# Weights joined in 16-bit pieces, loads of 112 rows, and one load issued later in a fused attention and gating kernel

## The chip, the cores and the metric

The kernel runs on one core of one Trainium2 chip. The metric is the device time of one execution in microseconds (us), the median of several runs; lower is better. The core has five engines that run side by side and meet at semaphores: PE (matrix products), DVE (vector), ACT (scalar functions), POOL and SP. SP issues all transfers of this kernel, in the order of its program, to 16 DMA engines.

## The reference

A linear attention with a decaying state feeds a gated layer that mixes over the positions of the sequence. Batch 4, 8 heads, 768 positions, head size 48, model width 384, inner width 1024.

```python
f = 1.0 / (1.0 + np.exp(-f_logit))
for t in range(S):
    state = f[:, :, t, :, None] * state + np.einsum('bhd,bhe->bhde', k[:, :, t], v[:, :, t])
    y[:, :, t] = np.einsum('bhd,bhde->bhe', q[:, :, t], state)
...
h = np.maximum(x @ w_in, 0.0)          # x: y with the heads side by side
u, v = h[..., :d_ff // 2], h[..., d_ff // 2:]
v_n = (v - mu) / np.sqrt(var + 1e-06)  # mean and variance over the width
v_s = np.einsum('ts,bsd->btd', w_spatial, v_n) + b_spatial[None, :, None]
return (u * v_s) @ w_out
```

## The kernel before

The sequence is cut into 24 units (4 batches by 6 stretches of 128 positions). For each unit n the attention needs f, k and q, which lie in one of three buffers `ins[n % 3]` (tile `fkq`), and v, in one of two (tile `val`). The two heads of a pair lie in rows 0 to 47 and 64 to 111 of the 128 rows of a buffer, so 112 rows are used. Products of float32 precision in the gated layer are made of a high and a low part of each factor, which takes three matrix products instead of one.

The order of all the work is written out by hand in the table `PLAN` (L44 to L115): each word is a step with its numbers, and a step's instructions go to the queues of their engines in the order of the words. Every engine works through its own queue in that order. So a word that is moved changes the order on the queue of each engine that it uses, and on no other.

The steps that matter here:

- `LF:n` (L350) loads f of unit n. For the first eight units f comes alone, as 128 positions by 384 (array `fn`); from unit 8 on one transfer brings f, k and q together. `LK:n` (L357) brings k and q of the first eight units. `LQ:n` (L361) loads v.
- `L:kind,i` (L291, written `LV`, `LU`, `LO` in the plan) loads one of six blocks of weights into a tile `words` or `late`. The weights were laid out as 64-bit integers, of which the kernel sees the low and the high 32-bit words (`parts_of`, L285): they are joined into a float32 on the chip.
- `ca` (ACT, L303) scales the high words into a third area t; `ct` (DVE, L308 to L310) then puts the bits together: it shifts the low words right by 29, shifts t left by 3 and combines it with the low words, and adds the sign bit of the high words. `ch` (ACT) and `cl` (DVE) make the high and the low part of the result.
- `k` (L399) and `q` (L403) on DVE scale k and q by the decays that `g` (L393) and `h` (L388) on ACT have made from the sums of f; `X` (L427, PE) makes the scores from them, `m` (L437, DVE) masks these, `YS` (L479, PE) multiplies them by v, and `kv` (L451, PE) adds to the state.

A load into a buffer has to wait until the earlier users of that part of it are done. SP carries these waits in its own queue: while one transfer waits there, all behind it wait as well.

For later use, the first words of the plan, and where `LK:3` stands:

```python
LF:0 constants kz LF:1 kq:1 c:0 e:0 LF:2 kq:0 c:1 LK:0 e:1 z:0 g:0 k:0 h:0 q:0 c:2 kj e:2 LV:1 z:1 LQ:0 ca:V,1
ct:V,1 X:0 w:0 h:1 g:1 LK:1 z:2 ch:V,1 m:0 k:1 YS:0 kv:0 q:1 LF:3 c:3 e:3 LV:0 r0:0 r1:0 X:1 w:1 cl:V,1 g:2 r2:0
Yq:0 z:3 fm:0 h:2 LQ:1 m:1 YS:1 kv:1 LK:3 LK:2 ys:0 k:2 q:2 ca:V,0 xt:0 X:2 LF:4 c:4 r0:1 LQ:2 r1:1 xh:0 xl:0
```

Of the kernel before, what the change touches and what calls it, by code (L numbers as in the profile page):

```python
# [11 lines left out]
F32R = mybir.dt.float32r  # L12
BF16 = mybir.dt.bfloat16
I32 = mybir.dt.int32
AF = mybir.ActivationFunctionType
ALU = mybir.AluOpType
PSUM = bass.MemoryType.PSUM

B, H, S, D = 4, 8, 768, 48
T = 128  # L20
C = 64
NU = S // T
N = B * NU
J = H // 2
DP = 112
# [4 lines left out]
P = 128  # L30
# [4 lines left out]
WB = 2 * DM  # L35
# [8 lines left out]
PLAN = """  # L44
    LF:0 constants kz LF:1 kq:1 c:0 e:0 LF:2 kq:0 c:1 LK:0 e:1 z:0 g:0 k:0 h:0 q:0 c:2 kj e:2 LV:1 z:1 LQ:0 ca:V,1
    ct:V,1 X:0 w:0 h:1 g:1 LK:1 z:2 ch:V,1 m:0 k:1 YS:0 kv:0 q:1 LF:3 c:3 e:3 LV:0 r0:0 r1:0 X:1 w:1 cl:V,1 g:2 r2:0
    Yq:0 z:3 fm:0 h:2 LQ:1 m:1 YS:1 kv:1 LK:3 LK:2 ys:0 k:2 q:2 ca:V,0 xt:0 X:2 LF:4 c:4 r0:1 LQ:2 r1:1 xh:0 xl:0
    e:4 z:4 m:2 g:3 LF:5 w:2 LK:4 r2:1 c:5 e:5 YS:2 kv:2 LQ:4 Yq:1 fm:1 h:3 ct:V,0 ys:1 ch:V,0 r0:2 q:3 z:5 g:5 g:4
    k:3 xt:1 LQ:3 LU:0 r1:2 cl:V,0 r2:2 xh:1 xl:1 X:3 w:3 Yq:2 ys:2 V:0,1 k:4 fm:2 h:4 LF:7 LF:6 q:4 X:4 m:3 YS:3
    c:6 kv:3 V:0,0 LK:5 ca:U,0 LU:1 ct:U,0 r0:3 w:4 ch:U,0 vr:0,1 xt:2 xh:2 m:4 YS:4 fm:3 r1:3 e:6 r2:3 vr:0,0 kv:4  # L50
# [107 lines left out]
def tile_kernel(ctx, tc, fkq, fn, vv, w_cv, w_spT, b_sp, out):  # L158
    nc = tc.nc
# [7 lines left out]
    def tiles(pool, name, count, shape, dtype=F32):  # L167
        return [pool.tile(shape, dtype, name=f"{name}{i}") for i in range(count)]
# [17 lines left out]
    ins = tiles(attn, "fkq", 3, [P, 3, J * T])  # L186
# [6 lines left out]
    sB = tiles(attn, "sB", 2, [DP, J * D])  # L193
    late_tile = const.tile([P, 3 * WB], I32, name="late")
    vr_tile = const.tile([P, HU, G], F32, name="vr")
# [6 lines left out]
    vns = Slots([tuple(const.tile([P, G], F32R, name=f"vn{k}{i}") for k in "hl") for i in range(6)])  # L202
    words = Slots(tiles(stage, "words", 2, [P, 3 * WB], I32))
    spat = Slots(tiles(stage, "spat", 2, [P, 2, TH]))
# [80 lines left out]
    def words_for(kind):  # L285
        return late if kind == "O" else words

    def parts_of(kind, i):
        w = words_for(kind).of((kind, i))
        low, high = (w[:, 0:2 * WB].rearrange("p (n two) -> p n two", two=2)[:, :, x] for x in range(2))  # L290
        return low, high, w[:, 2 * WB:]  # L291

    def step_L(kind, i):
        nc.sync.dma_start(
            words_for(kind).take((kind, i), 2)[:, 0:2 * WB].rearrange("p (h n) -> p h n", h=2),
            w_cv.bitcast(I32)["VUO".index(kind) * 2 + i].rearrange("h p n -> p h n"),
        )

    def step_ca(kind, i):


        low, high, t = parts_of(kind, i)
        nc.scalar.activation(t.bitcast(F32), high.bitcast(F32), AF.Copy, scale=2.0 ** -112)  # L303

    def step_ct(kind, i):

        low, high, t = parts_of(kind, i)
        nc.vector.tensor_scalar(low, low, 29, None, op0=ALU.logical_shift_right)  # L308
        nc.vector.scalar_tensor_tensor(t, t, 3, low, op0=ALU.logical_shift_left, op1=ALU.bitwise_or)
        nc.vector.scalar_tensor_tensor(t, high, -2 ** 31, t, op0=ALU.bitwise_and, op1=ALU.bitwise_or)  # L310

    def step_ch(kind, i):
        to, full = cols(kind, i)[0], view(kind, parts_of(kind, i)[2].bitcast(F32))
# [32 lines left out]
    def parts(n):  # L346
        t = ins[n % 3]
        return t[0:DP, 0], t[0:DP, 1], t[0:DP, 2]

    def step_LF(n):  # L350
        b, u = divmod(n, NU)
        if n < SUMMED:
            nc.sync.dma_start(ins[n % 3][:, 0, 0:HD], fn[n])
        else:
            nc.sync.dma_start(ins[n % 3], fkq[b, u])

    def step_LK(n):  # L357
        b, u = divmod(n, NU)
        nc.sync.dma_start(ins[n % 3][:, 1:3], fkq[b, u, :, 1:3])

    def step_LQ(n):  # L361
        b, u = divmod(n, NU)
# [6 lines left out]
    def step_e(n):  # L369
        f = ins[n % 3][:, 0, 0:HD] if n < SUMMED else parts(n)[0]  # L370
        nc.scalar.activation(f, f, AF.Exp, scale=-1.0)
        nc.scalar.activation(f, f, AF.Ln, bias=1.0)  # L372

# [10 lines left out]
    def sums(n):  # L384
        return mm.of(("z", n))[0:DP] if n < SUMMED else parts(n)[0]

    def step_h(n):
        nc.scalar.activation(Fs[n % 2], sums(n), AF.Exp, scale=-1.0)  # L388
        if n < SUMMED:
            mm.done(("z", n))  # L390

    def step_g(n):
        nc.scalar.activation(parts(n)[0], sums(n), AF.Exp)  # L393
        if n < SUMMED:
            mm.done(("z", n))
# [21 lines left out]
    low, high = slice(0, C), slice(C, P)  # L417
# [135 lines left out]
    def raw(b, u):  # L553
        if b not in WIN:
            return vrs.of((b, u))
        th, ut = divmod(u, HU)
        if (b, th) not in raws.held:
            raws.take((b, th), 4)
        return raws.of((b, th))[:, ut]
# [5 lines left out]
    def step_vr(b, u):  # L565
        th, ut = divmod(u, HU)
        sums = {"accum_out": half(b, th)["sum"][:, ut:ut + 1]} if moment(b, th) == "sums" else {}
        if b not in WIN:
            vrs.take((b, u))
        nc.scalar.activation(raw(b, u), mm.of(("v", b, u)), AF.Relu, **sums)  # L570
        mm.done(("v", b, u))
# [251 lines left out]
    count = const.tile([DP, 2], F32, name="count")  # L823
    bad = const.tile([1, 1], I32, name="bad")

# [54 lines left out]
    with tc.If(n_bad > 0) as found:  # L880
        xd = dram.tile([B, HD, S], F32, name="xd")
        with tc.tile_pool(name="steps", bufs=2) as sp:
# [5 lines left out]
            with tc.For_i(0, B) as b, tc.For_i(0, J) as j, tc.For_i(0, 2) as e:  # L888
                f, k, q = (sp.tile([D, NU, T], F32, tag="in", name="in", bufs=3) for _ in range(3))
# [7 lines left out]
                f, k, q = (t.rearrange("d u t -> d (u t)") for t in (f, k, q))  # L897
# [10 lines left out]
                for d in range(D):  # L908
                    kv = sp.tile([D, S], F32, name="kv")
# [101 lines left out]
```

## Time and profile before

| | |
|---|---|
| median of 3 runs | 344.37 us (343.79 to 344.56) |
| the profiled execution | 343.65 us |
| its span, first to last instruction | 341.9 us |
| PE busy | 327.2 us, 96% of the span |
| PE weight loads busy | 304.7 us |
| DVE busy | 251.3 us, 74% |
| ACT busy | 181.9 us, 53% |
| moved by DMA | 38.38 MB, 112 GB/s on the mean |

The span is the profiled execution without 1.7 us around it. PE is the engine with the most work, and its idle time is 14.7 us of the span. A share over the whole span hides where such idle time lies, so the rows below are taken by stretches. "issue" as a releaser means that the engine waited for nothing that the trace shows. A time in brackets at the end of a row is idle time of that engine in front of the row's first instruction, with what ended it.

### The profile page before, as it was taken

The page shows a single profiled execution, that of the slowest core. Times are in us where ns is not written, and L with a number is a line of the kernel's source. Part 1 is how long each engine was busy: PE and PEld are TensorE (multiplying, and loading weights), DVE is VectorE, ACT ScalarE, POOL GpSimd, SP SyncE. Part 2 cuts the span into 40 slices and gives each one's busy share as a digit, 9 for nine tenths or more (in the row PEclk, how much of TensorE's full clock was granted, in tenths as well). Part 3 has the DMA queues.
Part 4 walks back from the last instruction along what each step waited for, and adds up shares of the span by engine and source line. Part 5 has one row for each costly group of instructions (what it writes and reads, how often), then busy time and mean ns, then how long its engine had stood idle before and what let it go on. Part 6 is the DMA issues. An engine that isn't in the chain of part 4 may idle for free.

```text
span 341.9 us, 10491 instructions
## 1 busy us (share of the span) xinstructions
PE 327.2 (96%) x4554; PEld 304.7 (89%) x4554; DVE 251.3 (74%) x491; ACT 181.9 (53%) x369; POOL 48.2 (14%) x70
## 2 busy tenths in 40 slices
PE   4669999999999999999999999999999999999995
PEld 3557889889999999999999998899899899999995
DVE  2878888988988869765668557889998869624730
ACT  8665899685465745536435456443453444213431
POOL 3101200312120320051004042100101010001000
PEclk9999999999999999999999999999999999999998
DMA  7938578713454213243048121162200000011022
GB/s 253 353 97 269 182 271 304 252 30 138 143 157 134 83 54 110 77 157 117 2 143 265 46 85 50 46 200 104 71 1 0 2 0 0 2 46 49 23 74 98
DMA packets 16582, 38.38 MB, mean 112 GB/s; under 512 B 1552, under 2 KB 11792, under 8 KB 16528
## 3 DMA queue, kind: packets, MB, share of 16 engines
q1 hardware_dynamic: 16528, 37.62, 32.6%
q8 instruction: 38, 0.62, 0.8%
q14 instruction: 16, 0.13, 0.1%
HBM read 32.90 MB, written 4.72 MB: 110 GB/s over the span
## 4 chain that ended last, share of the span: by engine, by line
PE 93%; DMA 2%; issue 1%; DVE 1%; ACT 1%; SPq 0%; DVEq 0%
PE mm L658 15%; PE mm L644 12%; PE mm L542 12%; PE mm L797 10%; PE mm L733 7%; PE mn L733 6%; PE bp L427 6%; PE mn L797 5%; PE bp L479 4%; PE bp L491 4%; PE mn L542 3%; PE mn L644 3%; PE mm L504 3%; PE bp L451 3%; DMA words<-w_cv 2%; PE mm L382 2%
## 5 line engine op out<-in xcount | busy, mean ns | idle before, releaser
L399 DVE SCALAR_TENSOR_TENSOR fkq<-fkq 112x512 f32<-112x512 f32 x24 | 17.2, 718 | 11.4 <-ACT fkq L393 6.9
L649 ACT ACTIVATE uT<-mm 128x384 f32<-128x384 f32 x26 | 12.8, 491 | 22.8 <-PE mm L644 19.9
L779 ACT CAST gh<-uT 128x384 fp32r<-128x384 f32 x29 | 14.8, 514 | 18.3 <-DVE uT L775 13.6
L427 PE MATMUL bp<-q,fkq 48*64 48x112 f32 x768 | 23.7, 261 | 0.8 <-DVE q L403 0.6
L775 POOL TENSOR_TENSOR uT<-gt,uT 128x384 f32<-128x384 f32 x12 | 12.9, 1077 | 81.1 <-ACT uT L649 38.6
L470 POOL TENSOR_TENSOR sA<-sA,F 112x192 f32<-112x192 f32 x13 | 11.9, 916 | 85.4 <-DVE sA L465 81.2
L427 PEld LDWEIGHTS bp<-q,fkq 48*64 48x64 f32 x768 | 19.0, 133 | 4.7 <-DVE q L403 1.9
L377 DVE TENSOR_TENSOR_SCAN fkq<-runs,fkq 112x512 f32<-112x512 f32 x16 | 20.4, 1274 | 2.8 <-ACT fkq L372 2.8
L479 PEld LDWEIGHTS bp<-val,sc 64*64 64x64 f32 x768 | 14.2, 134 | 7.4 <-issue 3.5
L479 PE MATMUL bp<-val,sc 64*64 64x48 f32 x768 | 16.6, 220 | 4.1 <-DVE sc L437 2.1
L403 DVE TENSOR_TENSOR q<-fkq,F 112x512 f32<-112x512 f32 x24 | 16.5, 686 | 5.4 <-PE bp L491 4.0
L658 PE MATMUL mm<-w_sph,vnh 128*128 128x384 f32 x96 | 20.2, 345 | 0.0
L658 PE MATMUL mm<-w_sph,vnl 128*128 128x384 f32 x96 | 19.5, 338 | 0.0
L658 PE MATMUL mm<-w_spl,vnh 128*128 128x384 f32 x96 | 19.5, 338 | 0.0
L437 DVE TENSOR_TENSOR sc<-bp,mask 128x512 f32<-128x512 f32 x24 | 16.4, 683 | 3.8 <-PE bp L427 3.7
L644 PE MATMUL mm<-xTh,w_inh 128*128 128x384 f32 x78 | 18.9, 350 | 0.0
L367 POOL TENSOR_SCALAR fkq<-fkq 112x512 f32<-112x512 f32 (+1 forms) x8 | 12.4, 1550 | 40.7 <-DMA fkq<-fkq 20.6
L644 PE MATMUL mm<-xTl,w_inh 128*128 128x384 f32 x78 | 17.9, 338 | 0.0
L644 PE MATMUL mm<-xTh,w_inl 128*128 128x384 f32 x78 | 17.9, 338 | 0.0
L542 PE MATMUL mm<-w_inh,xTh 128*128 128x512 f32 x57 | 17.3, 411 | 0.0
L658 PEld LDWEIGHTS mm<-w_spl,vnh 128*128 128x128 f32 x96 | 17.1, 188 | 0.0
L658 PEld LDWEIGHTS mm<-w_sph,vnl 128*128 128x128 f32 x96 | 17.1, 188 | 0.0
(215 smaller groups left out, 900.3 us busy)
## 6 DMA issues: line engine op xcount, KB each, us to landing
fkq<-fkq SPq DMA_DIRECT2D x16, 768.0 KB, 4.9
val<-vv SPq DMA_DIRECT2D x24, 192.0 KB, 4.0
out<-osb SPq DMA_DIRECT2D x24, 192.0 KB, 2.1
fkq<-fkq SPq DMA_DIRECT2D x8, 512.0 KB, 5.7
words<-w_cv SPq DMA_DIRECT2D x4, 768.0 KB, 6.0
y<-w_spT SPq DMA_DIRECT2D x4, 576.0 KB, 5.9
fkq<-fn SPq DMA_DIRECT2D x8, 192.0 KB, 3.4
late<-w_cv SPq DMA_DIRECT2D x2, 768.0 KB, 5.9
```

Of the source, the lines that this page charges most:

```text
L377: return nc.vector.tensor_tensor_scan(f[0:DP], runs, f[0:DP], 0.0, op0=ALU.mult, op1=ALU.add)
L399: nc.vector.scalar_tensor_tensor(k, f, 1.0 / F_LEAST, k, op0=ALU.min, op1=ALU.mult)
L403: nc.vector.tensor_tensor(qs[n % 2][:, :, :, 0:C], *(x.rearrange("p (j c t) -> p j c t", c=T // C, t=C) for x in (parts(n)[2], Fs[n % 2])) ...
L427: nc.tensor.matmul(sc[to, e, cs], k[dr, at:at + C], qs[n % 2][dr, j, chunk], start=True, stop=True)
L437: nc.vector.tensor_tensor(Ss[n % 2].rearrange("p (e j t) -> p e j t", e=2, t=C), scores(n)[:, :, :, 0:C], mask.unsqueeze(1).unsqueeze(1).b ...
L479: nc.tensor.matmul(y[to, e, cs], s[rows, keys[e]], v[rows, hd], start=j == 0, stop=False, skip_group_check=True)
L542: nc.tensor.matmul(acc, xs[:, c, ut * P:(ut + 1) * P], ws[:, c, G:FF], start=i == 0, stop=i == 3 * KX - 1)
L644: nc.tensor.matmul(acc[:, 0:TH], ws[:, kx, cs], xs[:, kx, :], start=i == 0, stop=i == 3 * KX - 1)
L658: nc.tensor.matmul(acc[:, 0:TH], vns.of((b, ks))[va][:, cs], w_sp_s[wb][:, ks, th * TH:(th + 1) * TH], start=i == 0, stop=i == 3 * KS - 1,)
L733: nc.tensor.matmul(mm.of(user)[:, 0:TH], x, y, start=n == ks == 0 and i not in (3, 6, 7), stop=n == ks == 2, skip_group_check=True,)
L779: nc.scalar.copy(gs.take((b, th, c), HU)[0], uTs.of((b, th, c)))
L797: nc.tensor.matmul(acc[:, ms], gs.of((b, th, c))[ga][:, ts], w_out_s[wb][:, c, ms], start=c == cs[0] == 0 and ga == wb == 0, stop=c == cs[ ...
```

## The change

Three things change.

1. In `ct` the low 64-bit halves are seen as 16-bit pieces, four to a weight. Two one-source instructions write single pieces in place: the lowest piece becomes the second one shifted right by 13, and the second one becomes the sign bit of the highest. One two-source instruction then combines the 32-bit word made of these two pieces with t. Before, `ct` was one one-source instruction on 32-bit words and two two-source ones.
2. `LK:n`, and `LF:n` from unit 8 on, move 112 rows instead of 128; the array in memory has 112 rows per unit as well.
3. The word `LK:3` stands 12 words later, behind `LQ:2`.

```diff
-    Yq:0 z:3 fm:0 h:2 LQ:1 m:1 YS:1 kv:1 LK:3 LK:2 ys:0 k:2 q:2 ca:V,0 xt:0 X:2 LF:4 c:4 r0:1 LQ:2 r1:1 xh:0 xl:0
+    Yq:0 z:3 fm:0 h:2 LQ:1 m:1 YS:1 kv:1 LK:2 ys:0 k:2 q:2 ca:V,0 xt:0 X:2 LF:4 c:4 r0:1 LQ:2 LK:3 r1:1 xh:0 xl:0
...
     def step_ct(kind, i):
 
         low, high, t = parts_of(kind, i)
-        nc.vector.tensor_scalar(low, low, 29, None, op0=ALU.logical_shift_right)
+        pieces = words_for(kind).of((kind, i))[:, 0:2 * WB].bitcast(U16).rearrange("p (n four) -> p n four", four=4)
+        nc.vector.tensor_scalar(pieces[:, :, 0], pieces[:, :, 1], 13, None, op0=ALU.logical_shift_right)
+        nc.vector.tensor_scalar(pieces[:, :, 1], pieces[:, :, 3], 2 ** 15, None, op0=ALU.bitwise_and)
         nc.vector.scalar_tensor_tensor(t, t, 3, low, op0=ALU.logical_shift_left, op1=ALU.bitwise_or)
-        nc.vector.scalar_tensor_tensor(t, high, -2 ** 31, t, op0=ALU.bitwise_and, op1=ALU.bitwise_or)
...
         else:
-            nc.sync.dma_start(ins[n % 3], fkq[b, u])
+            nc.sync.dma_start(ins[n % 3][0:DP], fkq[b, u])
 
     def step_LK(n):
         b, u = divmod(n, NU)
-        nc.sync.dma_start(ins[n % 3][:, 1:3], fkq[b, u, :, 1:3])
+        nc.sync.dma_start(ins[n % 3][0:DP, 1:3], fkq[b, u, :, 1:3])
...
-        y = np.full((B, NU, P, J * T), pad, np.float32)
+        y = np.full((B, NU, DP, J * T), pad, np.float32)
```

On SP, from the third load of f alone into buffer 0 (`LF:3`) on, the queue stood like this before; `fkq0` to `fkq2` are the three buffers of f, k and q, `val` those of v, `words` those of weights, and 128x1024 is a load of k and q:

```order
L353 DMA fkq0_112<-fn 128x384
L294 DMA words1_160<-w_cv 128x2x768
L363 DMA val1_116<-vv 128x384
L359 DMA fkq0_112<-fkq 128x1024
L359 DMA fkq2_114<-fkq 128x1024
L353 DMA fkq1_113<-fn 128x384
L363 DMA val0_115<-vv 128x384
L353 DMA fkq2_114<-fn 128x384
L359 DMA fkq1_113<-fkq 128x1024
```

And the same place of SP's queue with the change (lines are numbered one or two higher):

```order
L355 DMA fkq0_112<-fn 128x384
L295 DMA words1_160<-w_cv 128x2x768
L365 DMA val1_116<-vv 128x384
L361 DMA fkq2_114<-fkq 112x1024
L355 DMA fkq1_113<-fn 128x384
L365 DMA val0_115<-vv 128x384
L361 DMA fkq0_112<-fkq 112x1024
L355 DMA fkq2_114<-fn 128x384
L361 DMA fkq1_113<-fkq 112x1024
```

The load of k and q of unit 3 into `fkq0` has moved from ahead of that of unit 2 (`fkq2`) to behind f of unit 4 and v of unit 2; the loads of k and q are 112 rows.

On DVE the first weights (`words0`) are joined just ahead of the mask of unit 0 (`sc0`) and of k and q of unit 1; before:

```order
L308 TENSOR_SCALAR words0_159<-words0_159 128x768
L309 SCALAR_TENSOR_TENSOR words0_159<-words0_159 128x768
L310 SCALAR_TENSOR_TENSOR words0_159<-words0_159 128x768
L437 TENSOR_TENSOR sc0_117<-bp0_138,mask_109 128x512
L399 SCALAR_TENSOR_TENSOR fkq1_113<-fkq1_113 112x512
```

With the change, in the same place of DVE's queue:

```order
L310 TENSOR_SCALAR words0_159<-words0_159 128x768
L311 TENSOR_SCALAR words0_159<-words0_159 128x768
L312 SCALAR_TENSOR_TENSOR words0_159<-words0_159 128x768
L439 TENSOR_TENSOR sc0_117<-bp0_138,mask_109 128x512
L401 SCALAR_TENSOR_TENSOR fkq1_113<-fkq1_113 112x512
```

One two-source instruction has gone and a one-source one has come; nothing else on DVE's queue moves. On PE, ACT and POOL the order is the same as before.

## Rows read from the trace of the kernel before

**Rows 1.** Busy us and instruction count of each engine, by three stretches

```profile
core 0: us, PE busy (x) PEld busy (x) DVE busy (x) ACT busy (x) POOL busy (x), PEclk, DMA share, GB/s
4.90:33.30 28.40, 22.52 (x608) 18.55 (x608) 21.20 (x37) 19.62 (x38) 4.23 (x7) 1.00 0.72 254
33.30:336.00 302.70, 302.50 (x3932) 284.13 (x3931) 228.60 (x450) 158.11 (x324) 41.80 (x51) 1.00 0.30 98
```

**Rows 2.** Chain that ended last, 0 to 90 us: start, us, what

```profile
2.65 7.09 DMA words<-w_cv
...
9.77 0.95 ACT words L303
...
12.63 0.68 DVE sc L437
...
17.55 1.64 issue
```

**Rows 3.** Timeline of DVE: start, us, instruction [idle before <-releaser]

```profile
9.77 0.56 DVE L308 TENSOR_SCALAR words<-words 128x768 int32<-128x768 int32 x1 [0.28 <-DMA words<-w_cv]
10.74 0.98 DVE L309 SCALAR_TENSOR_TENSOR words<-words 128x768 int32<-128x768 int32 x1 [0.41 <-ACT words L303]
11.76 0.96 DVE L310 SCALAR_TENSOR_TENSOR words<-words 128x768 int32<-128x768 int32 x1
...
17.55 0.69 DVE L399 SCALAR_TENSOR_TENSOR fkq<-fkq 112x512 f32<-112x512 f32 x1 [0.57 <-DMA fkq<-fkq]
...
22.45 0.56 DVE L308 TENSOR_SCALAR words<-words 128x768 int32<-128x768 int32 x1
23.04 0.96 DVE L309 SCALAR_TENSOR_TENSOR words<-words 128x768 int32<-128x768 int32 x1
```

**Rows 4.** Timeline of PE at its gaps

```profile
13.37 0.68 PE L479 MATMUL bp<-val,sc 64*64 64x48 f32 x32 [2.08 <-DVE sc L437]
...
17.11 0.43 PE L479 MATMUL bp<-val,sc 64*64 64x48 f32 x13
19.18 0.49 PE L479 MATMUL bp<-val,sc 64*64 64x48 f32 x18 [1.64 <-issue]
...
24.08 0.27 PE L479 MATMUL bp<-val,sc 64*64 64x48 f32 x5 [0.39 <-issue]
```

**Rows 5.** DMA packets by queue, 13.6 to 16.9 us

```profile
DMA packets 492, 1.28 MB, mean 388 GB/s; under 512 B 51, under 2 KB 256, under 8 KB 492
...
q1 hardware_dynamic: 492, 1.28, 98.5%
```

**Rows 6.** The same, 16.9 to 18.0 us

```profile
q8 instruction: 1, 0.02, 5.7%
```

**Rows 7.** The same, 21.7 to 22.7 us

```profile
q8 instruction: 1, 0.02, 5.8%
```

**Rows 8.** The same, 25.2 to 26.5 us

```profile
q8 instruction: 1, 0.02, 5.9%
```

**Rows 9.** SP's queue: start, us, issue

```profile
9.50 0.47 SPq L363 DMA_DIRECT2D val<-vv  x1
10.33 0.80 SPq L359 DMA_DIRECT2D fkq<-fkq  x2
...
14.47 0.33 SPq L363 DMA_DIRECT2D val<-vv  x1
18.27 0.33 SPq L353 DMA_DIRECT2D fkq<-fn  x1
18.70 0.38 SPq L359 DMA_DIRECT2D fkq<-fkq  x1
```

**Rows 10.** DMA packets, 5 to 10 us

```profile
DMA packets 656, 1.79 MB, mean 357 GB/s; under 512 B 61, under 2 KB 213, under 8 KB 656
```

**Rows 11.** DMA issues: size each, median us to landing (page)

```profile
fkq<-fkq SPq DMA_DIRECT2D x8, 512.0 KB, 5.7
```

**Rows 12.** Costliest groups: busy, mean ns (page)

```profile
L377 DVE TENSOR_TENSOR_SCAN fkq<-runs,fkq 112x512 f32<-112x512 f32 x16 | 20.4, 1274 | 2.8 <-ACT fkq L372 2.8
```

More of the change, by code (lines that the diff above doesn't have):

```diff
@@ L14 @@
 I32 = mybir.dt.int32
+U16 = mybir.dt.uint16
 AF = mybir.ActivationFunctionType
```

## The prediction

> **What bounds the kernel now.** I read the busy time by stretches first. From 33.3 to 336.0 us PE is busy for 302.5 of 302.7 us [rows 1]: there nothing but PE's own work counts, and the change touches none of it. Before, from 4.9 to 33.3 us, PE is idle for 5.9 us [rows 1]. So only what happens in the first 33 us can move the end, and a us that PE gains there is kept, as long as what feeds PE comes earlier by the same amount. It should: everything later waits for data, not for a time of day.
>
> Then the chain of waits. It leads through the load of the first weights, ACT's scaling of them and DVE's joining to the mask of unit 0 at 12.63, and further on through a gap of 1.64 us at 17.55 that has no releaser [rows 2]. DVE's timeline shows the first place close up: the weights are there at 9.77, the mask starts 2.86 us later [rows 2, 3], and PE's first product with v stood still for 2.08 us for it [rows 4].
>
> The second place needs another view. PE has two gaps put down to "issue", ending at 19.18 and 24.08, both in the middle of a run of equal products [rows 4], where no data can be missing. The packets by queue show a single packet of the instruction queue, 0.02 MB, beginning between 16.9 and 18.0 and another between 21.7 and 22.7 [rows 6, 7], so the restarts follow by 2.3 to 2.4 us at most; I work with these, that is with starts at 16.9 and 21.7. I take it that PE has run out of instructions and waits for the next page of its program. From 13.6 to 16.9 no such packet begins, and the data queue takes 98.5% of the engines' time [rows 5]: the page waits in line behind data. When is it asked for? The next page begins between 25.2 and 26.5 [rows 8], 1.1 us or more after PE started on a new page at 24.08 [rows 4], with little data about. So I read it as: a page is asked for when PE starts on the one before, and served after the data already queued on its engine.
>
> **The join.** Before, from weights to mask: 2.86 us. The first instruction ran beside ACT, the second waited 0.41 us for it [rows 3]. Now both piece instructions need the loaded words alone and can run beside ACT's 0.95 us [rows 2]; only the last one needs ACT. A one-source instruction over 768 words with a step of two words took 0.56 us and its successor began 0.59 us after it [rows 3]. With that price for each piece the last instruction starts at 1.18, past ACT's end, and the mask 0.87 us later (11.76 to 12.63 [rows 2, 3]): 2.05 us, a gain of 0.81. The trace has no 16-bit instruction. Bounds for a piece: 0.28 us, half of that row, if 16 bits went twice as fast; 1.91 us, if it were as slow per element as the slowest DVE group, 1274 ns for 512 [rows 12], times 768 over 512. I take 0.56, since the bytes that it steps over are those of the nearest row. At the 0.98 us of a two-source instruction [rows 3] the gain would be nothing.
>
> [...]
>
> Later joins (five more) are in stretches where PE hardly waits or not at all [rows 1]; there the gain of about 0.4 us of DVE time is hidden by PE's work and worth nothing.
>
> **112 rows.** A load of k and q shrinks from 512 KB [rows 11] by 64 KB. At 357 GB/s [rows 10] that is 0.18 us. Ahead of the first weights stands one of them; DVE had idled 0.28 us for these weights [rows 3], so all 0.18 count. Bounds: nothing, if the loads are set by something other than bytes, and also a loss of the same 0.18 if seven rows on each engine land worse than eight. With the join the mask starts 0.99 us earlier, at 11.64, and PE, whose work up to the first gap hangs on it, comes to the end of its page at 17.55 - 0.99 = 16.56.
>
> **The moved load.** Before, `LK:3` was issued at 10.33, ahead of `LK:2` [rows 9]. Now `LK:2` follows the load of v that ends at 9.97 [rows 9], and `LK:3` comes behind the issue of v that stood at 14.47 [rows 9], at about 13.9. SP does not wait there anew: the last readers of its buffer, the scores of unit 0, stand on PE ahead of the products with the old v, for whose end that load of v waits anyway. Ahead of the instruction page stand therefore 512 KB less for `LK:3` and three times 64 KB less for `LK:0`, `LK:1` and `LK:2`: 704 KB, 0.72 MB, at 388 GB/s [rows 5] 1.86 us. The page begins at about 15.05 instead of 16.9, and PE goes on at 17.3 instead of 19.18. It has come to the gap at 16.56, so it waits 0.75 us instead of 1.64. `LK:2` also lands earlier: DVE's wait of 0.57 us for it [rows 3] goes.
>
> What is late next is the page after. It is asked for at 17.3. By then queued are f of unit 4, v of unit 2, `LK:3`, f of unit 5 and probably `LK:4`, which SP issues 0.43 us after f of unit 5 [rows 9], when DVE has done k of unit 2. DVE was free for that at 17.55 - 0.57 and is now 0.99 earlier, at 15.99; with 0.69 us for k [rows 3] f of unit 5 goes out at 16.7 and `LK:4` at about 17.15, a hair ahead. From 15.05 on that engine serves the page (5.7% of 16 engines over 1.1 us, 1.0 us [rows 6]) and 1472 KB spread over all engines, 1.51 MB: 3.9 us at 388 GB/s, 4.2 at 357. So the second page begins at 19.95 to 20.25 instead of 21.7, and PE goes on 2.38 us later, at 22.35 to 22.65 instead of 24.08: 1.4 to 1.75 us earlier. If `LK:4` falls behind the request, PE finds its page there and keeps 1.86. I take 1.6. After 24.08 few loads are about and the rest moves with PE.
>
> The join and the shorter first load are thus mostly absorbed: what counts at 24.08 is when the pages come, and these hang on the bytes ahead.
>
> **Sum.** The profiled execution is 343.65 us with a span of 341.9; 1.6 less gives 342.05. Its median is 344.37, 0.72 above, so I say 342.8 for the median.
>
> **Rivals.**
>
> *Part of it only.* Either the loads of 112 rows are no shorter: then the gap at 17.55 is left 512 KB earlier, 0.52 MB at 388 GB/s, 1.35 us, and the next page stands behind 1600 KB, 1.64 MB: 15.55 + 1.0 + 4.2 = 20.75, PE at 23.1, 1.0 us gained. Or the gap at 17.55 is not the page's and keeps its 1.64 us: then PE gains the 0.99 of the mask alone. Both give 343.4. For it: "issue" names no releaser [rows 4]. Against it: two gaps with a packet shortly before each [rows 4, 6, 7]. [...]
>
> *The second page eats it.* `LK:3` now stands between the two pages instead of ahead of both. Should that engine need until 21.7 for the 1.51 MB, which is 267 GB/s, PE starts at 24.08 as before and all is lost: 344.4. For it: one engine that also carries pages can be slower than the mean. Against it: both stretches ran above 350 GB/s [rows 5, 10].
>
> *Slower.* The 16-bit pieces write two bytes in every eight. At 1.91 us a piece the join takes 3.82 + 0.87 = 4.7 us. The first one then brings PE to 17.55 + 1.65 = 19.2, as late as before. The second one, at 22.45, took 0.59 + 1.02 + 0.87 = 2.48 us [rows 2, 3]; it becomes 4.7 and sits on DVE ahead of q of unit 3, for which PE's scores wait: 2.2 us more, 346.6, and worse if the later joins hit as well. It decides from about 1.6 us a piece, where the second join loses what the pages gain.
>
> **Chances.** Forecast 0.50; part of it 0.22; second page 0.15; slower 0.10; 0.03 for what I don't see. 0.2%, 0.69 us, is about what a measurement of this kernel can tell from no change. The forecast and most of the partial case lie below 343.68: faster 0.70. The second page and the rest of the partial case: same 0.19. Slower 0.11. The forecast's own range is 342.2 to 343.4; to hold 8 in 10 I go from 341.8 to 344.4, which takes in most of the second page's case and leaves out the slower one.
>
> **What would show it.** In the profile after: each piece near 0.56 us; the mask of unit 0 at about 11.6; k of unit 2 without a wait for its load, near 16.0; the first gap with no releaser ending near 17.3, the second near 22.5; PE's idle time from 4.9 to 33.3 down from 5.9 to about 4.3, and nothing new from there on. I am wrong if the second gap still ends near 24, if a piece takes over 1 us, or if PE shows idle time behind 33 us.

## The result and the profile after

The changed kernel is slower: 348.92 us (median of 4 runs, 347.77 to 350.07) against 344.22 us for the kernel before (4 runs), a ratio of 1.0137 with a 95% interval of 1.0096 to 1.0179. I had forecast 342.8, and the time lies above my range. The profiled execution is the slowest of the four: it took 350.07 us with a span of 348.4, 6.5 us more than the span before.

First the same two stretches of time after the change; the columns are busy us and instruction count of each engine, then granted clock, DMA share and GB/s.

```profile
4.90:33.30 28.40, 24.51 (x535) 20.72 (x539) 20.77 (x35) 18.52 (x37) 4.23 (x7) 1.00 0.76 228
33.30:336.00 302.70, 299.57 (x3974) 279.63 (x3966) 230.11 (x449) 156.93 (x321) 42.09 (x51) 1.00 0.31 92
```

In the first stretch PE is busier than before [rows 1] with 73 fewer instructions: the same products take longer. In the second one it is now idle for 3.1 us instead of 0.2 [rows 1]. So there are two losses, one in each stretch, and the second is where I had seen nothing at risk.

DVE's timeline after (start, us, instruction, idle time before it) shows the first joining:

```profile
11.12 1.04 DVE L310 TENSOR_SCALAR words<-words 128x768 uint16<-128x768 uint16 x1 [1.11 <-DMA words<-w_cv]
12.19 1.04 DVE L311 TENSOR_SCALAR words<-words 128x768 uint16<-128x768 uint16 x1
13.34 0.96 DVE L312 SCALAR_TENSOR_TENSOR words<-words 128x768 int32<-128x768 int32 x1
14.21 0.68 DVE L439 TENSOR_TENSOR sc<-bp,mask 128x512 f32<-128x512 f32 x1
...
19.41 0.68 DVE L401 SCALAR_TENSOR_TENSOR fkq<-fkq 112x512 f32<-112x512 f32 x1
...
50.06 0.43 DVE L369 TENSOR_SCALAR fkq<-fkq 112x512 f32<-112x512 f32 x1 [1.29 <-DMA fkq<-fkq]
...
155.36 0.43 DVE L369 TENSOR_SCALAR fkq<-fkq 112x512 f32<-112x512 f32 x1 [2.53 <-DMA fkq<-fkq]
```

The first weights are there at 11.12 instead of 9.77 [rows 3]: the shorter load ahead of them did not let them land earlier, but 1.35 us later. A 16-bit piece takes 1.04 us instead of the 0.56 that I had taken, and the whole join 3.09 us instead of 2.86. The mask of unit 0 starts 1.58 us later than before. The last two rows lie behind 33 us: there DVE waits for a load of f, k and q. Behind the first of them PE stands 0.21 us for DVE, at 52.07, and behind the second 0.36 us for ACT, which had waited for DVE, at 157.53.

PE's timeline after:

```profile
9.79 1.77 PE L429 MATMUL bp<-q,fkq 48*64 48x112 f32 x32 [1.03 <-DVE q L405]
...
14.95 1.11 PE L481 MATMUL bp<-val,sc 64*64 64x48 f32 x32 [1.50 <-DVE sc L439]
...
22.42 1.00 PE L429 MATMUL bp<-q,fkq 48*64 48x112 f32 x32
...
25.98 0.27 PE L481 MATMUL bp<-val,sc 64*64 64x48 f32 x5 [0.35 <-issue]
...
121.45 0.73 PE L544 MATMUL mm<-w_inh,xTh 128*128 128x512 f32 x2 [0.77 <-ACT xTh L517]
```

The scores of a unit (32 products, L429) take 1.77 us at 9.79 and 1.00 at 22.42; the products with v took 0.68 us at 13.37 before [rows 4] and take 1.11 at 14.95 now. I read the longer times as a lower clock: in e3b the granted clock is 0.50 from 19 to 21 us, and there the products with v take 1.11 us too (19.79). The record of the granted clock has its first entry at 21.1 us, at full speed, where that of before has it at 8.8; ahead of the first entry the column in the windows shows 1.00, so the length of equal products is the better witness. The gap at 17.55 is gone, where I had forecast 0.75 us of it, but only because PE came to that place too late: its page, the packet of the instruction queue, begins at 18.15, and was to begin at about 15.05. The next one begins at 23.35, not at about 20, and the second gap ends at 25.98 instead of 24.08 [rows 4].

The chain that ended last now leads through loads of f, k and q (start, us, what):

```profile
43.85 6.19 DMA fkq<-fkq
...
112.42 4.78 DMA fkq<-fkq
117.34 2.37 POOL fkq L369
...
147.50 7.83 DMA fkq<-fkq
```

The chain of before has no load behind 30 us at all. And the page gives the loads a longer time for fewer bytes, in the table of issues (times, KB each, median us to landing), first before:

```profile
fkq<-fkq SPq DMA_DIRECT2D x16, 768.0 KB, 4.9
```

and after, with its line of the queue (packets, MB, share of 16 engines) ahead:

```profile
q1 hardware_dynamic: 16144, 35.53, 34.4%
...
fkq<-fkq SPq DMA_DIRECT2D x16, 672.0 KB, 5.5
...
fkq<-fkq SPq DMA_DIRECT2D x8, 448.0 KB, 6.0
```

Both kinds of load went up although an eighth of the bytes is gone: 4.9 to 5.5, and 5.7 [rows 11] to 6.0. 34.4% of a span of 348.4 us on 16 engines is 119.8 us; before it was 32.6% of 341.9, 111.5 us, for 37.62 MB.

To see where time is lost I followed the scores of each unit through the traces. The table gives the start of a unit's scores on PE minus its start before, in us (worked out from the timelines; these are units 2, 3, 5, 8, 11, 14, 16 and 20, with the time of before on top):

| start before | 20.5 | 26.7 | 40.9 | 58.4 | 96.2 | 125.6 | 153.7 | 193.3 | end of PE |
|---|---|---|---|---|---|---|---|---|---|
| after | 1.93 | 2.29 | 1.86 | 2.86 | 3.87 | 4.94 | 5.63 | 5.88 | 5.90 |
| e1, join | -0.79 | 0.60 | -0.30 | -0.11 | 0.13 | 0.13 | 0.16 | 0.13 | 0.70 |
| e2, 112 rows | 1.98 | 2.62 | 2.06 | 2.52 | 2.53 | 3.07 | 3.73 | 4.07 | 4.39 |
| e3b, moved load | 1.65 | 1.43 | 0.58 | 0.59 | 0.59 | 0.59 | 0.59 | 0.54 | 0.48 |
| e4, join and moved load | -1.76 | 0.40 | 0.86 | 0.87 | 1.21 | 1.31 | 1.37 | 1.37 | 1.67 |
| e6, late loads 112 rows | -0.89 | -0.19 | -1.30 | -0.98 | -0.28 | 0.29 | 0.35 | 0.62 | 1.19 |
| e7, early loads 112 rows | 2.73 | 3.28 | 3.18 | 3.19 | 3.26 | 3.25 | 3.23 | 3.16 | 3.65 |

Each row is one execution. e6 does the same as before up to its first late load, at 40.69 us, and is still 1.30 us away from it at 40.9: so far do single executions differ.

### The profile page after: what moved, and what is told of

It is laid out like the page before. It is cut to its first block, busy times and chain, and to the rows that moved or that the text cites. A ratio compares the mean times of both kernels' runs of the same rounds, so it can differ in the third digit from the quotient of the medians.

```text
span 348.4 us, 10489 instructions
## 1 busy us (share of the span) xinstructions
PE 332.2 (95%) x4554; PEld 308.3 (88%) x4554; DVE 254.1 (73%) x491; ACT 182.0 (52%) x369; POOL 48.5 (14%) x70
## 3 DMA queue, kind: packets, MB, share of 16 engines
q1 hardware_dynamic: 16144, 35.53, 34.4%
## 4 chain that ended last, share of the span: by engine, by line
PE 81%; DMA 9%; DVE 5%; ACT 2%; issue 1%; POOL 1%; SPq 1%; DVEq 0%; POOLq 0%
PE mm L646 11%; PE mm L544 11%; PE mm L799 10%; PE mm L660 8%; PE mm L735 6%; PE mn L735 6%; DMA fkq<-fkq 5%; PE bp L429 5%; PE mn L799 5%; PE bp L481 3%; PE bp L493 3%; PE mn L544 3%; PE mn L646 3%; DMA words<-w_cv 2%; PE bp L453 2%; PE mm L506 2%
## 5 line engine op out<-in xcount | busy, mean ns | idle before, releaser
L429 PE MATMUL bp<-q,fkq 48*64 48x112 f32 x768 | 25.3, 272 | 2.5 <-DVE q L405 1.8
L429 PEld LDWEIGHTS bp<-q,fkq 48*64 48x64 f32 x768 | 20.3, 140 | 6.5 <-DVE q L405 3.0
L781 ACT CAST gh<-uT 128x384 fp32r<-128x384 f32 x29 | 14.8, 514 | 18.3 <-DVE uT L777 13.6
L373 ACT ACTIVATE fkq<-fkq 112x512 f32<-112x512 f32 (+1 forms) x24 | 14.4, 599 | 7.8 <-POOL fkq L369 4.0
L384 PE MATMUL mm<-tri,fkq 128*48 128x128 f32 (+1 forms) x128 | 12.2, 352 | 5.5 <-ACT fkq L374 5.5
```

The costliest lines, as they stand in the source:

```text
L429: nc.tensor.matmul(sc[to, e, cs], k[dr, at:at + C], qs[n % 2][dr, j, chunk], start=True, stop=True)
L781: nc.scalar.copy(gs.take((b, th, c), HU)[0], uTs.of((b, th, c)))
```

## The experiments

### Each part alone

e1 is the first part of the change (the join in pieces), e2 the second (112 rows), e3 the third (the moved load), each alone on the kernel before. Cut to one line each, in this order:

```diff
+        nc.vector.tensor_scalar(pieces[:, :, 0], pieces[:, :, 1], 13, None, op0=ALU.logical_shift_right)
...
+        nc.sync.dma_start(ins[n % 3][0:DP, 1:3], fkq[b, u, :, 1:3])
...
-    ... kv:1 LK:3 LK:2 ys:0 ... LQ:2 r1:1 ...
+    ... kv:1 LK:2 ys:0 ... LQ:2 LK:3 r1:1 ...
```

> Before with the join in 16-bit pieces alone (128 rows, LK:3 in its old place). Theory A (the loads of 112 rows are what costs): the two pieces at about 1.04 us each make each join some 0.5 us longer than before; the first and second joins stand in front of work that PE waits for, so the kernel is 0.4 to 1.2 us slower, and there are no new waits of DVE or POOL for loads of f, k and q behind 45 us. Theory B (the join is what costs): 3 us or more slower, with PE idle in front of products that wait for DVE.

> Before with loads of 112 rows alone. Theory A: 3.5 to 5 us slower; the packets of 6144 bytes have a median near 0.32 us instead of 0.23, the loads of f, k and q land 0.5 us or more later though they are an eighth smaller, and DVE and POOL wait for them from 45 us on. Theory B: within 0.7 us of before.

> Before with LK:3 moved alone. By the prediction's account of instruction pages: the gap of PE at 17.55 with no releaser shrinks and the kernel is 0.8 to 1.9 us faster. If the page does not hang on the load moved: the gap keeps 1.6 us and the time is within 0.4 us of before. Theory C (the move is what costs): slower by over 1 us, with a wait for k and q of unit 3.

| | us | ratio to before | interval |
|---|---|---|---|
| e1, join | 344.79 | 1.0025 | 0.9997 to 1.0053 |
| e2, 112 rows | 348.76 | 1.0136 | 1.0086 to 1.0187 |
| e3, moved load | 344.02 | 0.9984 | 0.9957 to 1.0011 |

The loads of 112 rows alone cost as much as the whole change. The other two parts can't be told from no change here.

In e1 DVE and PE show why (DVE first):

```profile
10.01 1.05 DVE L310 TENSOR_SCALAR words<-words 128x768 uint16<-128x768 uint16 x1 [0.24 <-DMA words<-w_cv]
...
13.11 0.68 DVE L439 TENSOR_TENSOR sc<-bp,mask 128x512 f32<-128x512 f32 x1
...
22.41 0.36 DVE L369 TENSOR_SCALAR fkq<-fkq 128x384 f32<-128x384 f32 x1 [0.93 <-DMA fkq<-fn]
22.69 1.05 DVE L310 TENSOR_SCALAR words<-words 128x768 uint16<-128x768 uint16 x1
...
25.73 0.35 DVE L461 TENSOR_TENSOR sB<-bp,sA 112x192 f32<-112x192 f32 x1
```

```profile
27.34 1.00 PE L429 MATMUL bp<-q,fkq 48*64 48x112 f32 x32 [1.83 <-DVE fkq L401]
```

From weights to mask it is 3.10 us where it was 2.86 [rows 3], and the second join, ahead of q and k of unit 3, takes 3.04 us where it was 2.49 (22.45 to 24.94). PE then waits 1.83 us for k. Not all of that is the join: PE was 0.79 us early at unit 2, and DVE had itself stood 0.93 us for f of unit 5, at 22.41. The join's part is the mechanism of my slower rival at a smaller price: 0.55 us more for a join and not 2.2, and the loss stays below what e1's interval can show.

In e2 PE's first gap without a releaser is longer than in [rows 4], not shorter:

```profile
20.20 0.77 PE L479 MATMUL bp<-val,sc 64*64 64x48 f32 x18 [2.23 <-issue]
...
22.48 1.77 PE L427 MATMUL bp<-q,fkq 48*64 48x112 f32 x32
```

The packet of the page begins at 17.56, and before it began at 16.93. I read this as the page waiting behind the same loads, which are slower. After the gap the scores run at 1.77 us again: the clock is on record at full speed from 13.0 us on and at half from 19.9 to 26.7 us.

### What a piece costs

Five shifts of words that nobody reads any more follow each join in the kernel before, so that each form has its own line (319 to 323): 768 pieces side by side (a), every second piece (c), every fourth (d), 768 words side by side (e), 384 words, every fourth (g).

```diff
+        nc.vector.tensor_scalar(a, a, 13, None, op0=ALU.logical_shift_right)
+        nc.vector.tensor_scalar(c, c, 13, None, op0=ALU.logical_shift_right)
+        nc.vector.tensor_scalar(d, d, 13, None, op0=ALU.logical_shift_right)
+        nc.vector.tensor_scalar(e, e, 13, None, op0=ALU.logical_shift_right)
+        nc.vector.tensor_scalar(g, g, 13, None, op0=ALU.logical_shift_right)
```

> Before, and behind each join five one-source shifts in place on the dead low words, which leave the output as it is: 768 pieces of 16 bits side by side, with a step of two pieces, with a step of four; 768 words of 32 bits side by side, and 384 with a step of four words. If 16 bits with a gap are what makes a piece slow: about 0.35, 1.04 and 1.04 us, and 0.56 us for the words side by side. If the step of 8 bytes makes it slow: 0.56 us for a step of two pieces and 1.04 for four. The 384 words tell whether a step of 16 bytes slows 32-bit words: 0.36 us if not, more if so.

The groups by line (busy us, mean ns of one):

```profile
L319 DVE TENSOR_SCALAR words<-words 128x768 uint16<-128x768 uint16 x4 | 1.4, 361 | 0.1
L320 DVE TENSOR_SCALAR words<-words 128x768 uint16<-128x768 uint16 x4 | 2.5, 614 | 0.1
L321 DVE TENSOR_SCALAR words<-words 128x768 uint16<-128x768 uint16 x4 | 4.1, 1032 | 0.1
L322 DVE TENSOR_SCALAR words<-words 128x768 int32<-128x768 int32 x4 | 2.2, 560 | 0.1
L323 DVE TENSOR_SCALAR words<-words 128x384 int32<-128x384 int32 x4 | 2.0, 510 | 0.1
```

The number of elements is the same in the first three, and the price goes from 361 to 614 to 1032 ns with the step. Of words, 384 with a step of four cost nearly as much as 768 side by side. So the piece is dear because of its step. The row that I had taken (0.56 us) has a step of 8 bytes too, but in whole words, and so of two elements and not four. Counted in elements the two sizes come close: with a step of four a word costs 1.33 ns (510 for 384) and a piece 1.34 (1032 for 768), with a step of two 0.73 (558 for 768, in before) and 0.80.

### Is it the rows, or the layout in memory?

e5 loads 112 rows out of the array of 128 rows, here the loads of k and q, and in the same way those of f, k and q together. p1 runs ten loads of f, k and q one after another ahead of all work, with 128, 112, 96, 64 and 48 rows, twice over.

```diff
-        nc.sync.dma_start(ins[n % 3][:, 1:3], fkq[b, u, :, 1:3])
+        nc.sync.dma_start(ins[n % 3][0:DP, 1:3], fkq[b, u, 0:DP, 1:3])
...
+    def probe(r):
+        nc.sync.dma_start(ins[0][0:r], fkq[0, 0, 0:r])
...
+        for r in (P, DP, 96, 64, 48, P, DP, 96, 64, 48):
+            probe(r)
```

> Loads of 112 rows out of an array that keeps its 128 rows per unit. If the number of rows is what slows the loads: as the loads of 112 rows alone, 3.5 to 6 us slower than before. If the layout in memory is: within 1 us of before.

> Before, with ten loads of f, k and q of unit 0 in front, one after the other, each waiting for the one before: 128, 112, 96, 64 and 48 rows, twice. If time went by bytes, with about 2 us besides: 4.2, 3.9, 3.6, 3.1 and 2.8 us from issue to landing. If the engines get into each other's way with other than 128 rows: 112 rows take 0.2 us or more longer than 128, and 64 rows as long as 128.

e5 took 347.64 us, a ratio of 1.0103 (1.0027 to 1.0178): the rows cost without the smaller array in memory. The interval is too wide to say that the array costs nothing besides. The issues in p1 (times, KB each, median us to landing):

```profile
fkq<-fkq SPq DMA_DIRECT2D x2, 768.0 KB, 4.2
fkq<-fkq SPq DMA_DIRECT2D x2, 672.0 KB, 4.5
fkq<-fkq SPq DMA_DIRECT2D x2, 576.0 KB, 4.3
...
fkq<-fkq SPq DMA_DIRECT2D x2, 384.0 KB, 4.1
...
fkq<-fkq SPq DMA_DIRECT2D x2, 288.0 KB, 3.4
```

With nothing else about, a load of 112 rows takes 0.3 us longer than one of 128 (4.6 and 4.4 us against 4.1 and 4.2), and half the rows take nearly as long as all (4.4 and 3.9). The packets say the same: in a load of 128 rows three quarters of the packets of 6144 bytes took 234 ns, in one of 112 rows the median was 285 to 318 and in one of 64 rows 334 to 373.

The medians of 112, 96 and 64 rows lie within 0.3 us of that of 128, and 48 rows took 0.8 us less. The 2 us that I had put beside the bytes agree with the first loads of f in before: 192 KB landed in 2.5 us, and my estimate for their bytes is 0.55, at 357 GB/s [rows 10]. Why 112 rows take longer, and not only as long, no run here shows.

### A clock that rises earlier

Since the products take up to 1.8 times as long until 21 us after the change, I let PE run 12 products of zeros ahead of the first real ones, in the kernel before (w1) and with the moved load (w3).

```diff
-    LF:0 constants kz LF:1 kq:1 ... c:2 kj e:2 ...
+    LF:0 constants kz kj W0 D:12 W1 LF:1 kq:1 ... c:2 e:2 ...
```

> Before with 12 matrix products over zeros on PE ahead of the first real ones, while PE has nothing to do (the zeros are written earlier). [...]

> The moved load alone, with the same 12 products ahead. If the late rise of the clock ate the gain of the earlier instruction pages: the clock rises at 9 us or sooner, no gap of PE without a releaser is over 0.5 us from 13 to 25 us, and the time is 1.0 to 2.5 us under before. If the pages' gain is not there even so: the time is that of w1 within 0.4 us.

They were slower, where I had expected a gain or nothing: w1 347.68 us, 1.0109 (1.0067 to 1.0151), and w3 348.55 us, 1.0104 (1.0043 to 1.0165). The clock rose at 4.9 us in w1, but fell again after PE's idle time of 2.09 us ahead of 13.15, and with the additional instructions pages run out at other places: behind 33 us w1 has three gaps without a releaser, of 1.26, 0.85 and 0.90 us, and before has a single one, of 0.47, that ends at 33.02. PE's busy time by stretches and a gap in w1:

```profile
15.10:18.50 3.40, 3.40 (x56) 2.83 (x52) 2.10 (x4) 3.17 (x7) 1.21 (x2) 0.50 0.59 221
```

```profile
37.44 0.62 PE L542 MATMUL mm<-w_inh,xTh 128*128 128x512 f32 x2 [1.26 <-issue]
```

So this told nothing of what an early clock would be worth, and it gave no better kernel.

### The rest: do the parts add up?

e4 is the change without its 112 rows. e3b repeats e3. e6 has 112 rows only in the 16 loads of f, k and q together (from unit 8 on), e7 only in the eight of k and q, each on the kernel before; the first two lines are e6, the last two e7.

```diff
-            nc.sync.dma_start(ins[n % 3], fkq[b, u])
+            nc.sync.dma_start(ins[n % 3][0:DP], fkq[b, u, 0:DP])
...
-        nc.sync.dma_start(ins[n % 3][:, 1:3], fkq[b, u, :, 1:3])
+        nc.sync.dma_start(ins[n % 3][0:DP, 1:3], fkq[b, u, 0:DP, 1:3])
```

> The join in pieces and the moved load together, with all loads at 128 rows. Theory (the loads of 112 rows carry the whole loss of the changed kernel): between 343.5 and 345.5 us, about 344.5, ratio to before 0.999 to 1.005, no gap of PE behind 40 us with a load of k and q as its releaser, and a median packet of 6144 bytes as before. Rival (a part of the loss comes from the join and the move acting together, through the clock rising late): 346 us or more, ratio over 1.006.

> The moved load alone once more. Its first ratio was 0.9984 with 1 within its interval. Theory A (the instruction pages come earlier, but PE runs longer at the lower clock level, and the two cancel): ratio 0.998 to 1.001 again, 343.2 to 344.4 us. Theory B (the earlier pages leave a small gain): ratio at or below 0.998 with an interval below 1.

> The kernel before, with 112 rows only in the 16 late loads of f, k and q together (from unit 8 on); the eight early loads of k and q keep 128 rows. Theory (112 rows are slower per load, and the late loads make PE wait by themselves): PE's shift against before is 0 to 50 us and grows behind it by 2 to 4 us, 346 to 348 us. Rival (the late loads have slack enough, and the loss behind 50 us only follows from the late start): within 0.3% of before, 343.3 to 345 us.

> The complement: 112 rows only in the eight early loads of k and q, 128 rows in the late loads. Theory (each group of loads costs on its own, and the two add up to the 1.0136 of both together, of which the late ones took 1.0055): ratio about 1.008, 345.7 to 347.3 us, PE shifted by 2 to 3 us within the first 40 us and by little more behind it. Rival (the early loads only cost together with the late ones, which take up what the start lost): ratio below 1.003.

| | us | ratio to before | interval |
|---|---|---|---|
| e4, join and moved load | 345.40 | 1.0048 | 1.0018 to 1.0078 |
| e3b, moved load | 343.98 | 1.0004 | 0.9984 to 1.0024 |
| e6, late loads 112 rows | 345.25 | 1.0055 | 1.0029 to 1.0081 |
| e7, early loads 112 rows | 346.93 | 1.0081 | 1.0049 to 1.0113 |

The late and the early loads each cost on their own, and 1.0055 times 1.0081 is 1.0136, the ratio of e2. e6 lies below the 346 to 348 us that I had expected, but its interval is above 1. In the table of starts e6 loses 2.5 us from 40.9 us on, and e7 3.2 us ahead of it and 0.5 behind. e7's first gap shows the early loss (the same place as in [rows 4]):

```profile
20.95 0.77 PE L479 MATMUL bp<-val,sc 64*64 64x48 f32 x18 [3.00 <-issue]
```

Not all of it is the loads. The gap ends 1.77 us later than before, and from there to the scores of unit 3 e7 takes 9.06 us where before took 7.55: the other 1.5 us come behind the gap, with the clock on record at half from 20.1 to 27.0 us. In e6, with 128 rows there, the same gap is 1.00 us:

```profile
18.28 0.49 PE L479 MATMUL bp<-val,sc 64*64 64x48 f32 x18 [1.00 <-issue]
```

The first weights, whose load stands behind that of k and q of unit 0, are there at 9.49 to 10.58 us in the traces with 128 rows in the latter (before, e1, e3, e3b, e4, e6), at 10.19 to 11.88 with 112 (e2, e5, e7), and at 11.12 after.

e4 shows what became of the earlier pages. Its instruction pages begin at 14.99 and 18.54 us (where mine were to begin at 15.05 and about 20), PE has neither gap, and the scores of unit 2 start 1.76 us earlier than before. Then, DVE and after it PE:

```profile
22.23 0.36 DVE L369 TENSOR_SCALAR fkq<-fkq 128x384 f32<-128x384 f32 x1 [1.72 <-DMA fkq<-fn]
22.50 1.02 DVE L310 TENSOR_SCALAR words<-words 128x768 uint16<-128x768 uint16 x1
```

```profile
27.13 1.43 PE L429 MATMUL bp<-q,fkq 48*64 48x112 f32 x32 [1.81 <-DVE fkq L401]
```

f of unit 5 is issued at 17.58 and lands 4.6 us later. Before, it was issued at 18.27, landed 2.2 us later and lay ready when DVE took it up at 22.19. In e4 DVE is early and waits 1.72 us for the load, the join (now 3.02 us) comes behind it, and PE stands 1.81 us at the scores of unit 3; behind that the clock is on record at half from 27.6 to 31.0 us. All that the pages had brought is gone there. The moved k and q of unit 3 stand right ahead of this load, but e1 and e6, without the move, have 3.6 and 3.3 us for it, so what made it slower is open. e1 and e6 lose an early start at the same place: PE is 0.79 and 0.89 us early at unit 2, and in e6, with the old join, it stands 1.26 us for k of unit 3.

e3b shows the other way in which it goes. Both of its page gaps are gone too, but the clock falls. Windows of 2 us (the column ahead of the last two is the granted clock), and PE's scores of units 0, 1 and 2:

```profile
15.00:17.00 2.00, 1.84 (x54) 1.72 (x44) 1.97 (x5) 1.05 (x2) 0.60 (x1) 0.53 0.88 280
17.00:19.00 2.00, 2.00 (x31) 1.91 (x27) 1.39 (x4) 1.79 (x5) 0.61 (x2) 0.50 0.84 252
19.00:21.00 2.00, 2.00 (x58) 1.67 (x58) 0.88 (x3) 0.86 (x2) 0.00 (x0) 0.50 0.71 183
```

```profile
10.13 1.00 PE L427 MATMUL bp<-q,fkq 48*64 48x112 f32 x32 [1.49 <-DVE q L403]
...
15.37 1.77 PE L427 MATMUL bp<-q,fkq 48*64 48x112 f32 x32 [0.16 <-DVE q L403]
17.89 1.97 PE L382 MATMUL mm<-tri,fkq 128*64 128x128 f32 x16
19.79 1.11 PE L479 MATMUL bp<-val,sc 64*64 64x48 f32 x32
20.68 0.86 PE L451 MATMUL bp<-val,W 64*48 64x48 f32 x32
...
22.14 1.00 PE L427 MATMUL bp<-q,fkq 48*64 48x112 f32 x32
23.76 1.09 PE L382 MATMUL mm<-tri,fkq 128*64 128x128 f32 x16 [0.62 <-ACT fkq L372]
24.78 0.68 PE L479 MATMUL bp<-val,sc 64*64 64x48 f32 x32
25.28 0.54 PE L451 MATMUL bp<-val,W 64*48 64x48 f32 x32
```

From 15 to 21 us the clock is at half (0.53 and 0.50). The four groups there take 5.71 us and the same four behind 22 us take 3.31, so 2.4 us are lost to the clock, about the 2.03 of the two gaps of before [rows 4]. In e3 products took the longer time until 21 us too (those with v 1.11 us at 19.37, 0.68 at 24.16). Why the clock stayed up in the profiled execution of before, where PE was idle for 2.08 us ahead of 13.37 [rows 4], is not settled: in e3b PE was idle for 2.02 us ahead of 14.17, about as long.

What the clock costs over all runs is open too. The mean granted clock of each run is on record (it counts no loss ahead of its first entry). It is 0.995 or less in 4 of the 27 runs of before that were taken with e3b, e4 and e6, and in 8 of 12, 9 of 12 and 7 of 11 of theirs. In e4 and e6 these runs are longer than the rest (medians 345.5 against 343.7 and 345.8 against 344.5 us), in e3b hardly (344.0 against 343.9); the rest of before has 343.4. So a part of what e4 and e6 lose goes with a lower clock; whether the clock is its cause, or follows from longer waits, no run separates.

No version here is faster than the kernel before by more than its interval.

## Why the prediction was wrong

**The step that failed** is the term of the 112 rows: "At 357 GB/s that is 0.18 us", with bounds of nothing and "a loss of the same 0.18". I priced a load by its bytes. Alone a load of 112 rows takes 0.3 us more (p1), in the kernel 0.3 us more for k and q and 0.6 more for f, k and q. e2 puts 4.7 us on it (1.36% of 343.85). e6 and e7 share it out: 1.9 us for the late loads and 2.8 for the early ones. None of my rivals held it: the one that has the rows no shorter still gained, and the bound by which they land worse went into no rival. Why 112 rows land worse than 128 stays open.

**A second fault** lies in the same term. "The change touches none of it", I wrote of the time behind 33 us, but 16 of the 24 shortened loads belong there. I took PE's 302.5 of 302.7 us as proof that loads have no say; it only shows that they came in time. Such a load is issued when the last scores out of its buffer are done, and the kernel needs it not much later. In [rows 1] the slack is not visible, but the trace of before has it, as the landing of each load against its first use. Of the 16 late loads five land less than 0.2 us ahead of the instruction on DVE or POOL that takes them up, and two more 0.5 and 0.6 us ahead. One of these is the load of unit 8, issued at 41.99 and landed 4.3 us later:

```profile
46.82 0.42 DVE L367 TENSOR_SCALAR fkq<-fkq 112x512 f32<-112x512 f32 x1
```

After, the same load takes 6.19 us: 43.84 (end of the scores) to 50.06 is this load and nothing else on the chain. e6 prices the late loads at 0.55%, 1.9 us.

**The join.** The price of a piece was to be 0.56, bounds 0.28 and 1.91; it was 1.04. The gain of 0.81 at the mask of unit 0 became a loss of 0.24 (e1), the second and the fourth join are 0.55 and 0.56 longer, and the third, where DVE had stood for ACT before, 0.24. I had argued that the later joins are hidden by PE's work. The second one isn't once PE is early. My upper bound of 1.91 was too high and my row too low; p2's 361, 614 and 1032 ns stand in their place.

**The pages.** That PE waits in these gaps for a page holds. The 14 traces together have 25 gaps of PE over 0.3 us without a releaser, and in every one a packet of the instruction queue had begun 2.24 to 2.80 us ahead of the restart; a trace has 38 such packets. When a page comes I had only partly right. The first one begins at 15.95 to 16.93 with 128 rows and `LK:3` in its old place (before, e1, e6), at 14.82 to 16.34 with the load moved (e3, e3b, e4), and at 17.56 to 18.93 with 112 rows in the early loads (e2, e5, e7). So the move brings it about 1 us, where I had 1.86 with the shorter loads, the executions differ by as much, and the rows take more away: with both it begins at 18.15. The gap at this page is 0.36 to 1.64 us in before, e1 and e6, and 2.23 and 3.00 in e2 and e7.

**"The rest moves with PE"** failed where I left out two things. One is the load of f of unit 5: in e4 it lands at 22.2, and DVE and PE wait for it. I had put it ahead of the second page, but not asked when it lands. The other is that I took all of PE's durations from an execution whose clock was up from 8.8 us; without PE's gaps, but with the slower products until 21 us, PE is no further (e3, e3b).

**What was to show it.** k of unit 2 has no wait for its load, but at 19.41 instead of 16.0; the second gap ends at 25.98, not 22.5. Two of the three signs by which I said I would be wrong came true, a piece over 1 us and idle time behind 33 us, and the third was passed: the second gap does not end near 24 but later. The idle time from 4.9 to 33.3 fell to 3.9 us, below the 4.3 forecast, and means nothing, since slow products count as busy.

Whether the parts simply add is not settled: e2 times e4 is 1.0185, just above the interval of the change, but the intervals of e2 and e4 are wide enough for their product to lie within it. If they don't, what one part delays may hide what another would cost at the scores of unit 3; no run here separates that.

## What to carry to other kernels

Price a load by a measured load of the same number of rows, not by bytes, and count every load that the edit touches, also where the bound engine seems never to wait: its idle time shows waits, not slack. Slack is read load by load, from the landing to the first use. When a stall is taken out, look for the load that the next stretch needs and ask when that one lands. Idle time is comparable between two traces only if equal products take equally long in both.

## What the runs showed of the hardware

- Loads of 112 rows take longer than of 128: 4.5 against 4.2 us alone, 5.5 against 4.9 in the kernel; 64 rows take 4.1 alone (two loads of each size in p1).
- On DVE a one-source shift of 768 16-bit pieces takes 361 ns side by side, 614 with a step of two and 1032 with a step of four.
- PE stood for 0.35 to 3.00 us in gaps without a releaser, and went on 2.24 to 2.80 us after a packet of the instruction queue had begun; I read these gaps as waits for a page of instructions.
- In the first 22 us the time of equal products differs from run to run of the same kernel (e3 and e3b: scores of unit 0 in 1.77 and in 1.00 us). In e3b, where the granted clock is 0.53 from 15 to 17 us and 0.50 from 17 to 21, groups of products take 1.6 to 1.8 times as long there as behind 22 us (scores 1.77 against 1.00 us, products with v 1.11 against 0.68).
